# A two-layer decode kernel: chain pieces spread over the free steps, another closing block, and w2 loaded in rows of two

## The chip, the cores and the metric

The kernel runs on one core of a Trainium2 chip. A core has five engines with an instruction queue each: TensorE (PE: matrix products; its weight loads are listed as PEld), VectorE (DVE), ScalarE (ACT), GpSimd (POOL) and SyncE (SP, which issues nearly all transfers here). Data lies in HBM, is brought by 16 DMA engines into SBUF (128 partitions), and products are collected in PSUM banks. The metric is the device time of one execution in microseconds. Before the change it is 1165.13 us, the median of three runs (1164.89 to 1167.07).

## The reference

One token for each of 8 batch entries passes twice through an attention block and an MLP block, each with a layer norm ahead of it and a residual behind. Both passes use the same weights and the same caches.

```python
def _A_ref(x, k_cache, v_cache, wq, wo):          # B=8, D=512, 32 query heads, 8 KV heads, Sk=8192, Dh=128
    q = (x @ wq).reshape(B, Sq, Hq, Dh).transpose(0, 2, 1, 3)
    k = jnp.repeat(k_cache, rep, axis=1)
    v = jnp.repeat(v_cache, rep, axis=1)
    p = _softmax(jnp.einsum("bhqd,bhkd->bhqk", q, k) * (Dh ** -0.5), axis=-1)
    o = jnp.einsum("bhqk,bhkd->bhqd", p, v)
    return o.transpose(0, 2, 1, 3).reshape(B, Sq, Hq * Dh) @ wo

def _B_ref(x, w1, w2):                            # F=1792
    return jnp.einsum("bsf,fd->bsd", _silu(jnp.einsum("bsd,df->bsf", x, w1)), w2)

x = x + _A_ref(_layernorm(x), k_cache, v_cache, wq, wo)
x = x + _B_ref(_layernorm(x), w1, w2)
x = x + _A_ref(_layernorm(x), k_cache, v_cache, wq, wo)
x = x + _B_ref(_layernorm(x), w1, w2)
```

All of it is bf16. The two caches hold 134 MB each, so a pass over both is 268 MB.

## The kernel before

**Tasks and steps.** A task is the attention of one KV head group of one batch entry in one layer: 8192 keys, four query heads. There are 128 tasks, put in one order for the whole kernel by `make_tasks` (L159): layer 1 of a batch entry, later its layer 2, with tasks of other entries in between. A task has 8 steps of 1024 keys; the main loop (L918) runs over steps p. Each step transposes eight 128x128 blocks of K on TensorE (L538) and copies them back to SBUF on VectorE or ScalarE (L546, L544); every other step multiplies the queries with 2048 transposed keys (scores, L577), and the steps between multiply V with the probabilities (L643), 12 steps behind. Softmax lies between, on VectorE, GpSimd and ScalarE (L588 to L629), for each task at fixed steps.

**What is kept.** Five of the eight KV heads keep their transposed K in SBUF from layer 1 to layer 2, 20 blocks of 512 KB out of 28 slots; so the second layer loads less K. `plan_loads` (L200) fixes the order, the slot and the size (512 KB to 2 MB) of every load ahead of time, and the step after which its slot is free. SP issues them in this order (`issue_until`, L502), each behind a wait for the engines that last used the slot. The weights wo, w1 and w2 are loads in the same queue (L43, L505).

**The chain.** When the last layer-1 task of batch entry b is done, everything between its two attention layers follows in one chain of 22 pieces (`chain_of`, L828): the last two wo parts and the residual, seven pieces of the w1 products (L739) with the layer norm's operations beside them, the exponential and the Silu, four pieces of the w2 products with the residual, six pieces of the queries for three head groups with the second layer norm beside them, and the queries' scaling. The main loop takes one piece a step from this list (L942), as soon as there is one. Queries of the other five head groups (`asks`) follow only when the entry's layer-2 tasks have begun, and the wo parts of the next entry (`add_heads`) after that. The layer-2 tasks of entry b begin 30 steps after the chain's list is made, for the first and last entry 38.

**The layer norm in a chain** works on uncentered products and corrects them with column sums; its inverse root is a bit trick and three Newton steps on VectorE (`inverse_root`, L663).

**The closing** (`closing`, L776) does the last MLP for all eight entries at once: residual, sum over the features (VectorE and a GpSimd reduction over partitions, `total`, L684), centering, w1 products, centering again in fp32, square, second sum, inverse root in twelve VectorE operations, scaling, Silu, w2 products in four column quarters at once (`quads`, L780), and the store. `keep_busy` (L554) puts products of 512 columns on TensorE whose results nobody reads: four near the end of the last task (BEFORE) and six behind the w1 products (AFTER). A first Silu on a value that nobody reads (L789) makes ScalarE load the Silu table during the last task.

The planner's queue and the per-step order are all fixed when the kernel is built; the engines only wait on semaphores. `op` (L429) adds these waits by what an instruction reads and writes.

Of the kernel before, what the change touches and what calls it, by code (L numbers as in the profile page):

```python
# [9 lines left out]
LN_EPS = 1e-5  # L10
# [25 lines left out]
QSOON = 3  # L36
ASKS = (2, 5)
SUMS = 24
OPENING = 3
WEIGHTS = (("wo", 16), ("w1", 30), ("w2", 48))  # L40
NTP = 3
# [6 lines left out]
PVN = (12, 16)  # L48
CW = 32
AGAIN = 4  # L50
BEFORE, AFTER = 4, 6
ACT_EVAC = (0, 4, 6)

BF16 = mybir.dt.bfloat16
# [2 lines left out]
ACT = mybir.ActivationFunctionType  # L57
# [246 lines left out]
def _build(ctx, nc, A_x, A_k_cache, A_v_cache, A_wq, A_wo, B_w1, B_w2, out):  # L304
# [29 lines left out]
    def sb(shape, dt, name):  # L334
        _cnt[0] += 1
        return ctx.enter_context(nc.sbuf_tensor(f"{name}_{_cnt[0]}", shape, dt))
# [18 lines left out]
    w1_sb = sb([128, KT, F], BF16, "w1")  # L355
    w2_sb = sb([128, FT, D], BF16, "w2")
    ident = sb([128, 128], BF16, "ident")
    XT = [sb([128, KT, B], BF16, f"XT{n}") for n in range(3)]
    NQ = 128 // QUAD
    CPB = KB // 128  # L360
# [86 lines left out]
    def mm_group(steps, reads=(), writes=()):  # L447
        def run():
            inst = None
            for f in steps:  # L450
                inst = f()
            return inst
        return op(pe, run, reads, writes)
# [17 lines left out]
    with nc.Block() as block:  # L471

        @block.sync
        def _(sync_eng):
# [8 lines left out]
                ),  # L483
                reads=["ident"], writes=["ident"],
            )
            for n in range(NQB):
                op(pool, lambda n=n: pool.memset(QB[n], 0.0), writes=[f"QB{n}"])
            op(dve, lambda: dve.memset(one, 1.0), writes=["one"])
# [13 lines left out]
            def issue_until(pos):  # L502
                while queue and queue[0].after <= pos:
                    d = queue.pop(0)
                    if d.kind in weights:  # L505
                        src, dst = weights[d.kind]
                        dma(sp, dst[:, :, :], src.rearrange("(k p) n -> p k n", p=128), wsem[d.kind], writes=[d.kind])
                    else:
                        issue(d)

# [192 lines left out]

                return [lambda: total(xv, rx, 1), second] + inverse_root(1)

            def normed(xv, rx, w_sb, rw, outs, again=1):

                total(xv, rx, B)
                center(xbB, ["PT", "xb"], xv, rx, B)
                for f in project(w_sb, rw, outs, KT, lambda k: xbB[:, k, :], "xb", B, again=again):  # L710
                    f()
                if again > 1:
                    keep_busy(AFTER)
                center(xcB, ["xcB"], xv, rx, B)
                op(dve, lambda: dve.tensor_tensor(sqB, xcB, xcB, ALU.mult), reads=["xcB"], writes=["sqB"])
                total(sqB, "sqB", B)
                for f in inverse_root(B):
                    f()
# [7 lines left out]
            def project(w_sb, rw, outs, kparts, rhs_of, r_rhs, n, parts=1, again=1):  # L726

                steps = []
                w = CW if n == 1 else n * again

                def moved(k):
                    if n == 1:
                        return rhs_of(k).to_broadcast([128, w])
                    return rhs_of(k).unsqueeze(1).to_broadcast([128, again, n]) if again > 1 else rhs_of(k)

                for i, o in enumerate(outs):
                    for k in range(kparts):
                        steps.append(
                            lambda i=i, o=o, k=k: pe.matmul(  # L739
                                MISC[:, i * n:i * n + w] if again == 1 else  # L740
                                MISC[:, i * w:(i + 1) * w].rearrange("p (r b) -> p r b", b=n),
                                w_sb[:, k, o * 128:(o + 1) * 128], moved(k),
                                start=(k == 0), stop=(k == kparts - 1),
                            )
                        )
                cuts = [len(steps) * j // parts for j in range(parts + 1)]
                return [
                    lambda lo=lo, hi=hi: mm_group(steps[lo:hi], reads=[rw, r_rhs], writes=["MISC"])
                    for lo, hi in zip(cuts, cuts[1:])
                ]  # L750
# [24 lines left out]

            def closing(x0, x1, r0, r1):  # L776

                rows = SCp[0]

                def quads(lhs_of, rhs_of, parts, first, last):  # L780
                    return [
                        lambda k=k, c=c: pe.matmul(
                            rows[c * QUAD:c * QUAD + B, 0:128], lhs_of(k, c), rhs_of(k, c),
                            start=first, stop=last and k == parts - 1,
                        )
                        for k in range(parts) for c in range(KT)
                    ]

                op(act, lambda: act.activation(raw[:, 0:1], raw[:, 0:1], ACT.Silu), reads=["raw"], writes=["raw"])  # L789
                add_residual(x1, r1, x0, r0, B, B)  # L790
                mm_group(quads(lambda k, c: x1[:, c, :], lambda k, c: ident[:, :], 1, True, False),
                         reads=[r1, "ident"], writes=["SC0"])
                normed(x1, r1, w1_sb, "w1", range(FT), AGAIN)
                scaled(hB.rearrange("p (f b) -> p f b", b=B), ["P"], FT, AGAIN)
                op(act, lambda: act.activation(hsB, hB, ACT.Silu), reads=["P"], writes=["hsB"])
                mm_group(quads(lambda k, c: hsB[:, k * B:(k + 1) * B], lambda k, c: w2_sb[:, k, c * 128:(c + 1) * 128],
                               FT, False, True),
                         reads=["hsB", "w2"], writes=["SC0"])
                op(dve, lambda: dve.tensor_copy(P[:, 0:128], rows[:, 0:128]), reads=["SC0"], writes=["P"])
# [111 lines left out]
            setup = column_sums()  # L911
            chain_b = [None]
            turn = [0]
            last0 = {b: max(task_at[(0, b, g)] for g in range(HKV)) for b in range(B)}
            first1 = {b: min(task_at[(1, b, g)] for g in range(HKV)) * GPT for b in range(B)}
            ntask = len(tasks)

            for p in range(NG + LP + GPT + 1):  # L918
                tq = (p + LQ) // GPT
                if (p + LQ) % GPT == 0 and tq < ntask:  # L920
                    layer, b, _g = tasks[tq]
                    if layer == 1 and chain and chain_b[0] == b:
                        while chain:
                            chain.pop(0)()
                    emit_q(tq)
                emit_t_until(p + LT)
                if p % GPG == GPG - 1:
                    if p < NG:
                        emit_s(p)
                else:  # L930
                    for i in range(p - LP, p - LP + GPG):
                        if 0 <= i < NG:
                            emit_pv(i)
                ti, ph = p // GPT - 1, p % GPT
                if p == NG + 3:
                    keep_busy(BEFORE)
                if 0 <= ti < ntask and ph in soft:
                    for f in soft[ph]:
                        f(ti)
                if setup and p >= SUMS:  # L940
                    setup.pop(0)()
                elif chain:  # L942
                    left = max(1, first1[chain_b[0]] - EARLY - p)
                    for _n in range(2 if len(chain) > left else 1):
                        chain.pop(0)()
                elif asks and p >= first1[chain_b[0]]:
                    if p % GPT in ASKS:
                        asks.pop(0)()
                elif not setup and not asks and heads[turn[0]] and (p >= NG or turn[0] == B
                                         or p % GPG == GPG - 1 and (tasks[p // GPT][2], 0) in kept):  # L950
                    add_heads(turn[0])
                done = p - LP - GPT + GPG
                if done >= 0 and done % GPT == 0 and done // GPT < ntask:
                    tj = done // GPT
                    emit_norm(tj)
                    layer, b, _g = tasks[tj]
                    if layer == 0:
                        heads[b].append(_g)
                    elif b == B - 1:
                        heads[B].append(_g)  # L960
                    if layer == 0 and tj == last0[b]:
                        assert not setup and not chain and not asks and turn[0] == b
                        more, asks = chain_of(b)
                        chain.extend(more)
                        chain_b[0] = b
                        turn[0] = b + 1
                issue_until(p)
# [40 lines left out]
```

## Time and profile before

| | |
|---|---|
| median of three runs | 1165.13 us |
| the profiled execution: its time, its span | 1165.28 us, 1163.5 us |
| mean granted TensorE clock | 0.972 of full speed |
| TensorE busy / weight loads / VectorE / ScalarE / GpSimd | 83% / 65% / 51% / 33% / 10% |
| read from HBM | 465.05 MB, 400 GB/s over the span |
| last load of V lands, by the wait that it ends | 1152.3 us |

The span runs from the first to the last instruction. The slices show 40 equal parts of it, a digit for the busy share in tenths; a DMA share above 1 comes from packets that overlap on one engine. A row of the groups names line, engine, operation, output and inputs, shapes and count. In the timeline, the bracket says how long the engine was idle before the instruction and what ended it. In the stretches, the numbers behind the busy times are the granted clock, the DMA share and GB/s.

### The profile page before, as it was taken

The numbers are of one execution on the slowest core, as the hardware profiler recorded it, in microseconds if no ns is written. First come the engines' busy times: TensorE is split into PE (matmuls) and PEld (weight loads), VectorE is DVE, ScalarE is ACT, GpSimd is POOL, SyncE is SP. The second block draws the span as 40 slices with busy tenths as digits, with TensorE's granted clock in tenths as the row PEclk, the third lists the DMA queues.
The fourth block names the chain that finished last, engine by engine and source line by source line (L and its number), as shares of the span: only waits on it lengthen the run. The fifth ranks groups of instructions, "written<-read, shape, count | busy, mean of one in ns | idle before, by whom it ended". The sixth has DMA issues, their size and how long they took to land.

```text
span 1163.5 us, 44942 instructions
## 1 busy us (share of the span) xinstructions
PE 965.6 (83%) x19898; PEld 753.5 (65%) x19898; DVE 597.6 (51%) x1932; ACT 383.8 (33%) x660; POOL 118.1 (10%) x300
## 2 busy tenths in 40 slices
PE   4688887888878887989888887888879888888787
PEld 3577665677657665767666665667667666667565
DVE  2344564556545563556445654556446554556443
ACT  1223431343224331343234332343234322433232
POOL 0000011001100011001100111001100011001110
PEclk8789999999999999899999999999989998999998
DMA  9999999999999999999999999999999999999995
GB/s 367 388 418 402 406 405 413 423 400 404 412 423 414 387 405 419 420 393 407 410 420 409 397 405 422 415 396 404 403 422 413 395 408 421 419 392 397 410 411 212
DMA packets 100706, 467.98 MB, mean 402 GB/s; under 512 B 10520, under 2 KB 16416, under 8 KB 78624
## 3 DMA queue, kind: packets, MB, share of 16 engines
q1 hardware_dynamic: 100464, 465.09, 99.4%
q8 instruction: 157, 2.57, 0.9%
q14 instruction: 37, 0.30, 0.1%
q10 hardware_dynamic: 48, 0.01, 0.0%
HBM read 465.05 MB, written 0.01 MB: 400 GB/s over the span
## 4 chain that ended last, share of the span: by engine, by line
DMA 62%; PE 29%; DVE 3%; issue 2%; SPq 2%; ACT 2%; POOL 1%; ACTq 0%
DMA arena<-in_A_k_cache_dram 35%; DMA arena<-in_A_v_cache_dram 27%; PE TPp L538 10%; PE OTp L643 8%; PE SCp L577 5%; PE MISC L739 3%; SPq L443 2%; ACT P L602 2%; PE TPp L618 1%; PE MISC L758 1%; DVE small L588 1%; POOL small L592 1%; DVE PT L622 0%; DVE small L590 0%; DVE small L596 0%
## 5 line engine op out<-in xcount | busy, mean ns | idle before, releaser
L538 PE MATMUL TPp<-ident,arena 128*128 128x128 bf16 x5632 | 445.1, 223 | 86.1 <-DMA arena<-in_A_k_cache_dram 81.5
L546 DVE COPY arena<-TPp 128x1024 bf16<-128x1024 bf16 x440 | 303.8, 691 | 321.7 <-PE TPp L538 319.5
L538 PEld LDWEIGHTS TPp<-ident,arena 128*128 128x128 bf16 x5632 | 330.9, 99 | 154.1 <-DMA arena<-in_A_k_cache_dram 103.3
L544 ACT COPY arena<-TPp 128x1024 bf16<-128x1024 bf16 x264 | 267.0, 1012 | 305.2 <-PE TPp L538 305.2
L643 PE MATMUL OTp<-PT,arena 128*128 128x64 bf16 (+1 forms) x8192 | 317.4, 190 | 53.9 <-DMA arena<-in_A_v_cache_dram 31.0
L643 PEld LDWEIGHTS OTp<-PT,arena 128*128 128x128 bf16 x8192 | 273.6, 98 | 93.0 <-issue 48.0
L577 PE MATMUL SCp<-arena,QB 128*32 128x512 bf16 x2048 | 208.5, 397 | 10.0 <-DVE arena L546 4.3
L602 ACT ACTIVATE P<-SCp,small 128x512 bf16<-128x512 f32 x128 | 88.0, 687 | 387.8 <-DVE small L598 206.5
L592 POOL PARTITION_ALL_REDUCE small<-small x128 | 47.7, 373 | 713.9 <-DVE small L590 687.0
L588 DVE TENSOR_REDUCE small<-SCp 128x1 f32<-128x512 f32 x128 | 87.6, 684 | 40.2 <-PE SCp L577 39.2
L577 PEld LDWEIGHTS SCp<-arena,QB 128*32 128x32 bf16 x2048 | 54.1, 93 | 57.7 <-DVE arena L546 7.3
L610 POOL PARTITION_ALL_REDUCE small<-small x128 | 56.1, 438 | 236.3 <-DVE small L608 236.3
L622 DVE COPY PT<-TPp 128x256 bf16<-128x256 bf16 x128 | 37.3, 292 | 68.9 <-PE TPp L618 68.9
L618 PE MATMUL TPp<-ident,P 128*128 128x128 bf16 x512 | 51.2, 223 | 25.8 <-ACT P L602 25.8
L618 PEld LDWEIGHTS TPp<-ident,P 128*128 128x128 bf16 x512 | 29.1, 98 | 58.2 <-ACT P L602 44.5
L608 DVE TENSOR_SCALAR small<-small 128x4 f32<-128x4 f32 x128 | 29.2, 228 | 32.8 <-ACT P L602 32.2
L739 PE MATMUL MISC<-XT,wq 128*128 128x32 bf16 x1024 | 39.8, 177 | 1.0 <-issue 1.0
L739 PEld LDWEIGHTS MISC<-XT,wq 128*128 128x128 bf16 x1024 | 32.2, 96 | 8.4 <-issue 8.4
L758 PE MATMUL MISC<-at,wo 128*128 128x32 bf16 x1024 | 36.0, 177 | 1.6 <-issue 1.5
L758 PEld LDWEIGHTS MISC<-at,wo 128*128 128x128 bf16 x1024 | 31.6, 96 | 5.1 <-issue 5.1
L590 DVE SCALAR_TENSOR_TENSOR small<-small 128x4 f32<-128x4 f32 x128 | 28.5, 223 | 4.5
L596 DVE SCALAR_TENSOR_TENSOR small<-small 128x4 f32<-128x4 f32 x128 | 20.0, 156 | 20.4 <-POOL small L592 20.4
(69 smaller groups left out, 322.4 us busy)
## 6 DMA issues: line engine op xcount, KB each, us to landing
arena<-in_A_v_cache_dram SPq DMA_DIRECT2D x290, 512.0 KB, 8.3
arena<-in_A_v_cache_dram SPq DMA_DIRECT2D x111, 1024.0 KB, 11.4
arena<-in_A_k_cache_dram SPq DMA_DIRECT2D x192, 512.0 KB, 8.2
arena<-in_A_k_cache_dram SPq DMA_DIRECT2D x24, 2048.0 KB, 15.0
arena<-in_A_k_cache_dram SPq DMA_DIRECT2D x32, 1024.0 KB, 14.8
wq<-in_A_wq_dram SPq DMA_DIRECT2D x1, 4096.0 KB, 16.8
wo<-in_A_wo_dram SPq DMA_DIRECT2D x1, 4096.0 KB, 27.8
w<-in_B_w_dram SPq DMA_DIRECT2D x2, 1792.0 KB, 26.8
```

What stands on the lines that cost most here:

```text
L538: lambda c=c: pe.transpose(tpv[:, c, :], chunk(slot, h * GRP + c), ident[:, :])
L544: op(act, lambda: act.copy(dst, TPp[tb][:, :]), reads=[f"TP{tb}"], writes=[r_half(slot, h)])
L546: op(dve, lambda: dve.tensor_copy(dst, TPp[tb][:, :]), reads=[f"TP{tb}"], writes=[r_half(slot, h)])
L577: lambda c=c: pe.matmul(SCp[bank][c * QUAD:(c + 1) * QUAD, :], QB[qn][:, NGRAN - 1 - k:NGRAN - 1 - k + QUAD], ARENA[:, slot * SLOT + c * K ...
L588: op(dve, lambda: dve.tensor_reduce(rowmax, SCp[bank][:, :], AX.X, ALU.max), reads=[f"SC{bank}"], writes=["rowmax"])
L592: op(pool, lambda: pool.partition_all_reduce(tops, top, 128, bass.bass_isa.ReduceOp.max), reads=["top"], writes=["tops"])
L602: op(act, lambda: act.activation(P[:, :], SCp[bank][:, :], ACT.Exp, bias=shift, scale=SM_SCALE, accum_out=rs[st]), reads=[f"SC{bank}", "sh ...
L610: op(pool, lambda: pool.partition_all_reduce(ssa[st], ssm[st], 128, bass.bass_isa.ReduceOp.add), reads=[f"ssm{st}"], writes=[f"ssa{st}"])
L618: lambda c=c: pe.transpose(tpv[:, c, :], P[:, c * 128:(c + 1) * 128], ident[:, :])
L643: lambda c=c, cc=cc: pe.matmul(otp, chunk(slot, h * GRP + c), pv[:, cc % CPB, cc // CPB % NQ, k, :].unsqueeze(2).to_broadcast([128, REP, w ...
L739: lambda i=i, o=o, k=k: pe.matmul(MISC[:, i * n:i * n + w] if again == 1 else MISC[:, i * w:(i + 1) * w].rearrange("p (r b) -> p r b", b=n ...
L758: lambda o=o, h=h: pe.matmul(MISC[:, o * w:(o + 1) * w], wo_sb[:, h, o * 128:(o + 1) * 128], rhs_of(h).to_broadcast([128, w]) if n == 1 el ...
```

## The change

Three things are changed.

The main loop counts, when a chain begins, the steps left until two before the entry's first layer-2 task, and takes so many pieces at each step that they are spread evenly: 22 pieces over 27 steps, or over 35 for the first and the last entry.

The closing block takes the means from TensorE: x1 is multiplied with a block of ones, which a memset writes over a used part of wq at step NG + 1. The variance is the mean of squares minus the square of the mean; ScalarE squares, VectorE and GpSimd sum. The inverse root is exp(-0.5 ln v) on ScalarE, with a table set that holds both functions and is loaded at the kernel's start. The Silu table is loaded behind them. `keep_busy` has two products ahead of w1 and three behind it.

w2 comes into SBUF so that each partition gets two neighbouring rows of w2 (2 KB) at a time: 7 x 128 pieces of 2 KB instead of 14 x 128 of 1 KB. The hidden features then lie in another order, so the w1 products read every second column of w1.

```diff
+FC = 2
+LN_EXP = 6
-BEFORE, AFTER = 4, 6
+BEFORE, BETWEEN, AFTER = 4, 2, 3
...
+    ones = wq_sb[:, KT - 1, 0:128]
...
+            act.add_instruction(mybir.InstLoadActFuncSet(
+                name=nc.get_next_instruction_name(), act_func_set_id=LN_EXP, ins=[], outs=[]))
...
+                        if d.kind == "w2":
+                            dst = dst[:, :, :].rearrange("p (a c) d -> p a (c d)", c=FC)
+                            src = src.rearrange("(a p c) d -> p a (c d)", p=128, c=FC)
...
+                def columns(k, o):
+                    if rw == "w1":
+                        lo = o // FC * FC * 128 + o % FC
+                        return w_sb[:, k, lo:lo + FC * 127 + 1:FC]
+                    return w_sb[:, k, o * 128:(o + 1) * 128]
...
-                op(act, lambda: act.activation(raw[:, 0:1], raw[:, 0:1], ACT.Silu), reads=["raw"], writes=["raw"])
                 add_residual(x1, r1, x0, r0, B, B)
+                mm_group([lambda k=k: pe.matmul(means[:, 0:B], ones[:, :], x1[:, k, :], start=(k == 0), stop=(k == KT - 1))
+                          for k in range(KT)], reads=[r1, "wq"], writes=["SC1"])
                 mm_group(quads(lambda k, c: x1[:, c, :], lambda k, c: ident[:, :], 1, True, False),
                          reads=[r1, "ident"], writes=["SC0"])
-                normed(x1, r1, w1_sb, "w1", range(FT), AGAIN)
+                op(act, lambda: act.activation(sqB, x1, ACT.Square), reads=[r1], writes=["PT", "sqB"])
+                op(dve, lambda: dve.tensor_reduce(s1, sqB.rearrange("p k b -> p b k"), AX.X, ALU.add),
+                   reads=["sqB"], writes=["s1"])
+                op(pool, lambda: pool.partition_all_reduce(s1a, s1, 128, bass.bass_isa.ReduceOp.add),
+                   reads=["s1"], writes=["s1a"])
+                keep_busy(BETWEEN)
+                op(dve, lambda: dve.scalar_tensor_tensor(
+                    xbB, means[:, 0:B].unsqueeze(1).to_broadcast([128, KT, B]), -1.0 / D, x1, op0=ALU.mult, op1=ALU.add),
+                   reads=["SC1", r1], writes=["PT", "xb"])
+                project(w1_sb, "w1", range(FT), KT, lambda k: xbB[:, k, :], "xb", B, again=AGAIN)[0]()
+                keep_busy(AFTER)
+                op(act, lambda: act.activation(tr, means[:, 0:B], ACT.Square, scale=1.0 / D), reads=["SC1"], writes=["tr", "SC1"])
+                op(dve, lambda: dve.scalar_tensor_tensor(s1a, s1a, 1.0 / D, tr, op0=ALU.mult, op1=ALU.subtract),
+                   reads=["s1a", "tr"], writes=["s1a"])
+                op(dve, lambda: dve.tensor_scalar(s1a, s1a, 0.0, LN_EPS, op0=ALU.max, op1=ALU.add),
+                   reads=["s1a"], writes=["s1a"])
+                op(act, lambda: act.activation(tr, s1a, ACT.Ln), reads=["s1a"], writes=["tr"])
+                op(act, lambda: act.activation(yr, tr, ACT.Exp, scale=-0.5), reads=["tr"], writes=["yr"])
+                op(act, lambda: act.activation(raw[:, 0:1], raw[:, 0:1], ACT.Silu), reads=["raw"], writes=["raw"])
                 scaled(hB.rearrange("p (f b) -> p f b", b=B), ["P"], FT, AGAIN)
...
+                if p == NG + 1:
+                    op(dve, lambda: dve.memset(ones, 1.0), writes=["wq"])
...
                     left = max(1, first1[chain_b[0]] - EARLY - p)
-                    for _n in range(2 if len(chain) > left else 1):
+                    span[0] = max(span[0], left)
+                    for _n in range(max(0, len(chain) - span[1] * (left - 1) // span[0])):
                         chain.pop(0)()
...
+                        span[:] = [0, len(chain)]
```

More of the change, by code (lines that the diff above doesn't have):

```diff
@@ L506, in issue_until @@
                         src, dst = weights[d.kind]
[L507 removed]
+                        if d.kind == "w2":
+                            dst = dst[:, :, :].rearrange("p (a c) d -> p a (c d)", c=FC)
+                            src = src.rearrange("(a p c) d -> p a (c d)", p=128, c=FC)
+                        else:
+                            dst, src = dst[:, :, :], src.rearrange("(k p) n -> p k n", p=128)
+                        dma(sp, dst, src, wsem[d.kind], writes=[d.kind])
                     else:
@@ L704, in ln_stages, with normed @@
                 return [lambda: total(xv, rx, 1), second] + inverse_root(1)
-            def normed(xv, rx, w_sb, rw, outs, again=1):
+            def normed(xv, rx, w_sb, rw, outs):
                 total(xv, rx, B)
                 center(xbB, ["PT", "xb"], xv, rx, B)
-                for f in project(w_sb, rw, outs, KT, lambda k: xbB[:, k, :], "xb", B, again=again):
+                for f in project(w_sb, rw, outs, KT, lambda k: xbB[:, k, :], "xb", B):
                     f()
-                if again > 1:
-                    keep_busy(AFTER)
                 center(xcB, ["xcB"], xv, rx, B)
@@ L741, in project @@
                                 MISC[:, i * w:(i + 1) * w].rearrange("p (r b) -> p r b", b=n),
-                                w_sb[:, k, o * 128:(o + 1) * 128], moved(k),
+                                columns(k, o), moved(k),
                                 start=(k == 0), stop=(k == kparts - 1),
@@ L776, in closing @@
             def closing(x0, x1, r0, r1):
-                rows = SCp[0]
+                rows, means = SCp
                 def quads(lhs_of, rhs_of, parts, first, last):
@@ L913, in _ @@
             turn = [0]
+            span = [0, 0]
             last0 = {b: max(task_at[(0, b, g)] for g in range(HKV)) for b in range(B)}
```

## The prediction

> **What bounds the kernel now.** I read the page from the top: busy shares first, then the slices.
>
> ```profile
> PE 965.6 (83%) x19898; PEld 753.5 (65%) x19898; DVE 597.6 (51%) x1932; ACT 383.8 (33%) x660; POOL 118.1 (10%) x300
> ...
> DMA  9999999999999999999999999999999999999995
> ...
> q1 hardware_dynamic: 100464, 465.09, 99.4%
> ```
>
> TensorE is busy 83% of the span, but the DMA engines are full in every slice except the last. So the question is whether loads are ever short of requests. The DMA issues of the page give the depth of the queue:
>
> ```profile
> arena<-in_A_v_cache_dram SPq DMA_DIRECT2D x290, 512.0 KB, 8.3
> ...
> arena<-in_A_k_cache_dram SPq DMA_DIRECT2D x192, 512.0 KB, 8.2
> ```
>
> 512 KB at 408 GB/s take 1.29 us, and a load lands 8.2 us after its issue: some six loads are under way at any time. Next, stretches of the span: one ahead of a chain (the rows of line L739 with w1 put the chain of the second batch at 270 us), three with a chain in them, one behind a chain.
>
> ```profile
> core 0: us, PE busy (x) PEld busy (x) DVE busy (x) ACT busy (x) POOL busy (x), PEclk, DMA share, GB/s
> 225.00:265.00 40.00, 35.41 (x688) 28.05 (x689) 22.01 (x56) 16.56 (x25) 3.44 (x9) 1.00 1.01 405
> 270.00:298.00 28.00, 24.86 (x559) 20.14 (x556) 18.91 (x77) 10.13 (x17) 3.59 (x9) 1.00 1.02 404
> 425.00:465.00 40.00, 30.86 (x689) 22.33 (x685) 18.14 (x67) 8.37 (x21) 4.83 (x12) 0.99 1.02 416
> 657.00:683.00 26.00, 23.30 (x528) 18.93 (x525) 16.75 (x70) 10.08 (x16) 3.19 (x8) 1.00 1.03 405
> 1045.00:1072.00 27.00, 24.02 (x548) 19.67 (x546) 17.76 (x73) 10.06 (x16) 3.32 (x9) 1.00 1.03 402
> ```
>
> A chain adds work to TensorE and VectorE (18.91 us of VectorE in 28, against 22.01 in 40), and the DMA share stays above 1.00 at the rate of the stretch ahead of it. Up to the last load the time is bytes over rate. The last load lands at 1152.3 us; what follows is serial, and the timeline shows it:
>
> ```profile
> start us, us, engine line op out<-in xcount [idle before <-releaser]
> ...
> 1152.36 0.57 PE L643 MATMUL OTp<-PT,arena 128*128 128x48 bf16 x16 [0.67 <-DMA arena<-in_A_v_cache_dram]
> ...
> 1153.82 0.19 DVE L770 TENSOR_TENSOR XT<-MISC,XT 128x32 bf16<-128x32 f32 x1 [0.68 <-PE MISC L758]
> ...
> 1154.35 0.41 POOL L687 PARTITION_ALL_REDUCE small<-small  x1 [4.37 <-DVE small L685]
> ...
> 1155.04 1.68 PE L739 MATMUL MISC<-PT,w 128*128 128x32 bf16 x56 [0.69 <-DVE PT L691]
> ...
> 1156.09 0.17 DVE L668 TENSOR_SCALAR small<-small 128x8 f32<-128x8 f32 x1 [0.54 <-POOL small L687]
> ...
> 1158.90 0.30 ACT L795 ACTIVATE PT<-P 128x112 bf16<-128x112 f32 x1 [8.20 <-DVE P L721]
> ...
> 1159.25 1.67 PE L782 MATMUL SCp<-w,PT 128*8 128x128 bf16 x56
> ```
>
> Between 1154.01 (end of the residual) and 1159.25 (start of the w2 products) VectorE sets the pace: two reductions through GpSimd and twelve small operations of 0.17 us at a pitch of 0.20 for the inverse root (1156.09 to 1158.49), then scaling, Silu. The w1 products were done at 1156.72 and waited.
>
> **The change, part by part.** The sum is made against the profiled execution: span 1163.54, time 1165.28 (1.74 lie around the span), 0.15 above the median of 1165.13.
>
> *The spread.* Before, a chain's 22 pieces took one step each from the step after the last wo part became known; now they lie over 27 steps (batches 1 to 6) or 35 (batches 0 and 7). No piece is added: every matmul, VectorE operation and the two GpSimd reductions of each layer norm stay, in the same order among themselves, later against the transposes and softmax. SP's order is unchanged, and each load's wait names transposes, scores or PV work, not the chain. The last piece (queries of the first groups) comes 4 steps before its layer-2 task instead of 8 (16 for the long ones), some 5 us by a step of 1.3 (a chain's seven w1 pieces span 8.1 us); it needs 0.22 + 0.24 us of VectorE, so ScalarE's copy into QB finds it done. Price: 0. What hides it is the queue of six loads, 8 us deep; with that cover gone, up to a step of 1.3 us per batch could show, 10 us in all. From the other side: if the chain stretches ran at the 416 GB/s of the stretch behind, 8 x 27 us x (1 - 404/416) = 6.2 us would be gained. I take 0, since the nearest row, the stretch ahead without a chain, has 405.
>
> *w2 in rows of two.* 1,792 packets of 1 KB become 896 of 2 KB. The row of the stretch where w2 passes:
>
> ```profile
> 84.00:87.00 3.00, 2.70 (x64) 2.37 (x65) 2.14 (x7) 0.78 (x2) 0.37 (x1) 1.00 1.02 426
> 87.50:93.50 6.00, 5.00 (x122) 4.30 (x119) 1.76 (x4) 2.46 (x4) 0.34 (x1) 1.00 1.08 365
> ```
>
> The slices inside it, where only w2 passes, show 349 GB/s: 1.835 MB take 5.26 us. At the 405 of 4 KB packets they would take 4.53. By packet, sixteen at a time, 1 KB costs 46.9 ns and 4 KB 162 ns; the line between gives 85 ns for 2 KB, 4.77 us in all. Gain 0.49; ends 0 and 0.73. The engines are full there, so it moves the last load by as much.
>
> *The stride in w1.* To match, the w1 columns of a hidden block are read two apart, in the 504 w1 weight loads of setup and chains and the 56 of the closing. The trace has no strided weight load. Its rows with 128 columns in a row step by 26.7 ns a pair (w1 at 1155.04: 56 in 1.50 us plus 0.18 of drain). Bounds: 26.7, and four times that, 107 ns. I take 26.7: the same 26.7 stands under clock 1.00 (L758, 8 columns moved) and 0.50, so the read has a pace of its own, and the nearest row is the same load without stride.
>
> [...]
>
> *Small edits.* ScalarE's table load moves to the start, where ScalarE waits 5.1 us for the first K: 0. The memset of 128x128 for the ones (GpSimd's like it: 0.20 us) stands on VectorE between L590 and L596, under the 0.37 us of the GpSimd reduction at 1147.57, five us ahead of the last load: 0.
>
> *The closing,* from the residual's end at 1154.01, with gaps as in the timeline (VectorE to TensorE 0.05, to GpSimd 0.09, others 0.03 to 0.04):
> - ScalarE squares x1 (32 elements; 14 take 0.215, 112 take 0.296): 0.23, to 1154.28. VectorE waits for it with its reduction (0.21, to 1154.52), and the centering queued behind waits too: 0.20, to 1154.75. GpSimd: 0.41, from 1154.61 to 1155.02.
> - TensorE: four products with ones, four with the identity, then two fillers of 0.427 (their pitch at clock 0.50) from about 1154.28: they end at 1155.13, later than the centering. So w1 starts at 1155.13, 0.09 later than before, and its results are there at 1156.8.
> - ScalarE squares the means behind the centering (PSUM bank SC1 is held for it): to 1154.99. VectorE: two operations, to 1155.42. Ln and Exp at 0.21: to 1155.90. That replaces a second reduction and twelve operations.
> - The Silu table load (1.28, row L789) was hidden at 1149.2 and now stands behind Exp: 1155.92 to 1157.20, and the first Silu to 1157.42.
> - Scaling is done at 1157.10 (w1 + 0.28), so it waits for ScalarE; Silu ends at 1157.75. The three fillers behind w1 end at 1157.90 at clock 0.50. w2 starts at 1157.80 to 1157.90 instead of 1159.25: gain 1.34.
>
> *The clock.* In this execution the granted clock was 0.50 in the whole closing:
>
> ```profile
> 1154.00:1157.40 3.40, 2.64 (x63) 1.91 (x64) 2.02 (x13) 0.00 (x0) 0.82 (x2) 0.50 0.00 0
> 1157.40:1160.80 3.40, 3.40 (x61) 1.79 (x59) 1.19 (x7) 0.30 (x1) 0.00 (x0) 0.50 0.00 0
> ...
> 464.50:467.90 3.40, 2.74 (x32) 2.11 (x33) 2.01 (x6) 0.00 (x0) 0.37 (x1) 0.50 1.02 431
> 467.90:471.30 3.40, 3.40 (x41) 2.77 (x39) 1.13 (x4) 1.77 (x3) 0.43 (x1) 0.50 0.98 405
> 471.40:474.70 3.30, 3.30 (x72) 2.74 (x70) 1.76 (x4) 1.11 (x2) 0.00 (x0) 1.00 1.04 437
> ```
>
> It changes in steps of 3.41 us, and a stretch at 0.50 that is 3.40 busy is followed by 1.00, one with 2.64 or 2.74 is not. The two fillers close the gap from 1154.35 to 1155.04, so the stretch from 1154.0 becomes about 3.3 busy and the clock should be back at 1157.4, ahead of w2. The w2 products are 14 rounds of 107 ns at 0.50 and of 53 ns at 1.00: 0.75 less. The sum: 0.49 + 1.34 + 0.75 = 2.58, 1165.28 - 2.58 = **1162.7 us**.
>
> **The rivals.** Measurement tells 0.2% (2.3 us) from no change, so small terms decide the sign.
> 1. *The clock's steps fall otherwise.* Then w2 stays at 0.50: 1165.28 - 1.83 = 1163.4, within 0.2%. For it: a step needs to begin within about 1 us of 1154.1, out of 3.41. Against: in the profiled execution it did. [...]
> 2. *The spread does move the stream,* at half of the 6.2 us above: about 1159.6. For it: TensorE waits 81.5 us for K over the run. Against: DMA share above 1.00 in every chain stretch.
> 3. *Strided weights at 53 ns.* w1 ends at 1155.13 + 2.97 + 0.18 = 1158.28, w2 starts at 1159.0: gain 0.25 there, 0.49 from w2: 1164.5, within 0.2%.
> 4. *Slower: strided weights at 107 ns.* w1 ends at 1161.3, w2 starts at 1162.0, 2.75 late; less 0.49 is +2.3; each chain holds TensorE 56 x 80 ns = 4.5 us longer, half the queue, and a microsecond per two batches gets through: 4. About 1171. Up to 34 ns a pair costs nothing (w1 done by 1157.1), from 68 ns the closing and w2 gain nothing. For it: no row shows such loads.
>
> **Chances.** Forecast 0.36 (its own range 1161.8 to 1163.6; 0.28 beyond 0.2%, 0.08 within), rival 1 0.25 (0.06 beyond, 0.19 within), rival 2 0.12 (faster), rival 3 0.10 (within), rival 4 0.17 (slower, a starved stream by the spread included). Faster 0.46, same 0.37, slower 0.17. The range 1161.0 to 1165.0 takes in rivals 1 and 3 and leaves out 4 and most of 2.
>
> **What would show it.** The last load lands 0.5 us earlier (1151.8) with chain stretches still at 402 to 408 GB/s; w1's 56 loads take 1.5 us; the ACT table load stands at about 2.9 us behind the last PV; from the residual's end to the start of w2 it takes 3.8 us instead of 5.2. It is wrong if w1 steps by more than 34 ns, if the DMA share drops below 1.00 in a chain, or if the Silu table load ends later than 1.3 us behind Exp.

## The result

The changed kernel takes 1164.41 us (median of 22 runs, 1162.40 to 1167.86) against 1166.46 us for the kernel before in the same sessions (22 runs, 1164.82 to 1168.17): ratio 0.9984, 95% interval 0.9979 to 0.9990, so 1.9 us less, between 1.2 and 2.4. Measured again later beside another set of runs of the kernel before, the ratio was 0.9993 (0.9984 to 1.0001); the two intervals overlap, and the change is worth about 0.07% to 0.16%. The profiled execution took 1165.14 us with a span of 1163.32.

The page of the changed kernel, the lines that answer to those of before:

```profile
PE 970.5 (83%) x19898; PEld 758.8 (65%) x19901; DVE 594.6 (51%) x1920; ACT 384.6 (33%) x664; POOL 117.5 (10%) x299
...
DMA  9999999999999999999999999999999999999996
...
q1 hardware_dynamic: 99568, 465.09, 99.4%
...
arena<-in_A_v_cache_dram SPq DMA_DIRECT2D x290, 512.0 KB, 8.0
...
arena<-in_A_k_cache_dram SPq DMA_DIRECT2D x192, 512.0 KB, 8.2
```

The shares are the same, the packets are 896 fewer, and a load of 512 KB still lands some 8 us after its issue. Stretches of the changed kernel (columns as before: busy times, granted clock, DMA share, GB/s), first the one in which w2 passes:

```profile
core 0: us, PE busy (x) PEld busy (x) DVE busy (x) ACT busy (x) POOL busy (x), PEclk, DMA share, GB/s
87.50:93.50 6.00, 4.73 (x114) 4.08 (x112) 1.84 (x5) 2.12 (x3) 0.43 (x1) 1.00 1.05 398
...
225.00:265.00 40.00, 35.35 (x700) 28.26 (x698) 22.26 (x56) 16.91 (x27) 3.20 (x8) 1.00 1.02 407
270.00:298.00 28.00, 24.24 (x534) 19.48 (x531) 17.41 (x66) 10.16 (x16) 3.59 (x9) 1.00 1.02 401
...
425.00:465.00 40.00, 31.82 (x701) 23.25 (x702) 17.73 (x73) 8.37 (x21) 4.83 (x12) 0.97 1.02 417
661.00:687.00 26.00, 23.42 (x524) 18.86 (x522) 17.14 (x64) 10.05 (x16) 3.59 (x9) 1.00 1.00 382
1048.00:1075.00 27.00, 23.01 (x502) 18.38 (x498) 17.04 (x61) 9.94 (x18) 2.79 (x7) 1.00 1.03 408
```

With w2 the rate is 398 instead of 365 GB/s. With a chain it is 401 and 408, where it was 404 and 402. One chain stretch stands out: 661 to 687 ran at 382 GB/s with a DMA share of 1.00, where the kernel before had 405 and 1.03 (657 to 683). Just ahead of it the granted clock was 0.50, from 656.84 to 660.26. In the second profile of the changed kernel the same stretch has 398 GB/s at 1.02, and with the spread alone 403 at 1.02. So the slow stretch is one profile's, and the two others with the same spread do not have it. The closing, in the timeline of the changed kernel:

```profile
start us, us, engine line op out<-in xcount [idle before <-releaser]
...
1155.90 0.19 DVE L785 TENSOR_TENSOR XT<-MISC,XT 128x32 bf16<-128x32 f32 x1 [0.68 <-PE MISC L773]
1156.12 0.23 ACT L809 ACTIVATE PT<-XT 128x32 f32<-128x32 bf16 x1 [5.01 <-DVE XT L785]
...
1156.68 0.41 POOL L812 PARTITION_ALL_REDUCE small<-small  x1 [4.79 <-DVE PT L815]
...
1156.93 1.56 PE L754 MATMUL MISC<-PT,w 128*128 128x32 bf16 x56
1157.12 0.17 DVE L821 SCALAR_TENSOR_TENSOR small<-small 128x8 f32<-128x8 f32 x1 [0.43 <-POOL small L812]
...
1157.53 0.21 ACT L825 ACTIVATE small<-small 128x8 f32<-128x8 f32 x1 [0.57 <-DVE small L823]
1157.77 0.21 ACT L826 ACTIVATE small<-small 128x8 f32<-128x8 f32 x1
1157.99 1.28 ACT L827 ACT_TABLE_LOAD   x1
...
1159.40 0.28 ACT L829 ACTIVATE PT<-P 128x112 bf16<-128x112 f32 x1
1159.73 0.95 PE L797 MATMUL SCp<-w,PT 128*8 128x128 bf16 x56 [0.58 <-ACT PT L829]
```

One reduction on GpSimd instead of two, then Ln, Exp, the Silu table load, Silu. From the residual's end (1156.09) to the start of the w2 products it takes 3.64 us, before 5.23. The products take 0.95 us instead of 1.67, since the granted clock is 1.00 in the whole closing here. The last load lands 2.1 us later than in the execution shown of before (1154.4 against 1152.3), which eats most of that in this one execution; the last section comes back to it.

### The profile page after: what moved, and what is told of

It is laid out like the page before. It is cut to its first block, busy times and chain, and to the rows that moved or that the text cites. A ratio compares the mean times of both kernels' runs of the same rounds, so it can differ in the third digit from the quotient of the medians.

```text
span 1163.3 us, 44939 instructions
## 1 busy us (share of the span) xinstructions
PE 970.5 (83%) x19898; PEld 758.8 (65%) x19901; DVE 594.6 (51%) x1920; ACT 384.6 (33%) x664; POOL 117.5 (10%) x299
## 4 chain that ended last, share of the span: by engine, by line
DMA 64%; PE 25%; DVE 3%; issue 2%; SPq 2%; ACT 2%; POOL 1%; POOLq 0%; ACTq 0%
DMA arena<-in_A_k_cache_dram 33%; DMA arena<-in_A_v_cache_dram 31%; PE TPp L548 9%; PE OTp L653 8%; PE SCp L587 4%; SPq L446 2%; ACT P L612 2%; PE MISC L754 2%; PE TPp L628 1%; DVE small L598 1%; PE MISC L773 1%; POOL small L602 1%; DVE small L600 0%; DVE PT L632 0%; DVE arena L556 0%
## 5 line engine op out<-in xcount | busy, mean ns | idle before, releaser
L548 PEld LDWEIGHTS TPp<-ident,arena 128*128 128x128 bf16 x5632 | 334.6, 100 | 152.3 <-DMA arena<-in_A_k_cache_dram 101.1
```

The costliest lines, as they stand in the source:

```text
L548: lambda c=c: pe.transpose(tpv[:, c, :], chunk(slot, h * GRP + c), ident[:, :])
```

## The experiments

Each kernel ran beside the kernel before; ratios are to that kernel's runs on the same chip, with a 95% interval.

### The spread alone

The kernel before with the changed lines of the main loop.

```diff
-                    for _n in range(2 if len(chain) > left else 1):
+                    span[0] = max(span[0], left)
+                    for _n in range(max(0, len(chain) - span[1] * (left - 1) // span[0])):
```

> The kernel before with the spread of the chain alone. If the transfers bound everything up to the last load (my theory): ratio 0.9995 to 1.0005, the closing as before (5.2 us from the residual's end to the start of the w2 products, if the clock is at 0.50), chain stretches at 400 to 408 GB/s. If the spread moves the stream (rival 2): ratio 0.997 to 0.9985, that is 2 to 3 us, and the last load lands earlier by as much. If the later end of the chain costs something: ratio over 1.001.

Measured: ratio 1.0005 (0.9996 to 1.0013). The gain of 2 to 3 us of rival 2 lies outside the interval. The closing took 5.21 us to the start of w2, as before. The stretches of this kernel with chains:

```profile
270.00:298.00 28.00, 24.11 (x535) 19.40 (x532) 17.37 (x65) 10.16 (x16) 3.46 (x9) 1.00 1.02 400
400.00:426.00 26.00, 23.68 (x528) 19.20 (x524) 17.11 (x65) 10.16 (x16) 3.22 (x8) 1.00 1.03 408
```

The spread is worth nothing that this interval shows.

### The chain crowded: two and four pieces at each step

Is that because placement never matters, or because one piece a step is already mild enough? The opposite edit, on the kernel before:

```diff
-                    for _n in range(2 if len(chain) > left else 1):
+                    for _n in range(min(len(chain), 4)):
```

> The kernel before with up to four pieces of a chain at each step instead of one, so that the 22 pieces stand within 6 steps. If the six loads under way hide any placement of the chain: ratio 0.9995 to 1.001 and a DMA share of 1.00 or more in the chain stretches. If placement matters, this is the harsher case: some 6 us of waits and products pile up in each of 8 chains, 2 to 4 us a chain get past the queue: ratio 1.01 to 1.03.

Measured: 1.0367 (1.0348 to 1.0385), 1208.07 us: 42 us more, 5.3 per chain, over the 2 to 4 expected if placement matters. And with 2 in place of 4:

> The kernel before with two pieces of a chain at each step, 11 steps, between one a step (before) and four (1.0367 measured). If there is a sharp edge where the queue runs dry: two a step still fits, ratio 0.9995 to 1.003. If the cost grows with the crowding: some 14 us, ratio 1.008 to 1.016.

Measured: 1.0208 (1.0186 to 1.0231), 1190.83 us: 25 us more, 3.1 per chain, above both expectations. One chain of each, first four pieces a step, then two:

```profile
275.00:280.00 5.00, 3.55 (x102) 3.02 (x98) 3.67 (x21) 1.01 (x1) 0.80 (x2) 1.00 1.01 392
280.00:285.00 5.00, 3.73 (x109) 3.30 (x110) 2.24 (x12) 0.76 (x3) 0.38 (x1) 1.00 0.78 278
285.00:290.00 5.00, 4.04 (x106) 3.49 (x102) 4.13 (x18) 0.55 (x1) 0.76 (x2) 1.00 0.70 220
```

```profile
275.00:280.00 5.00, 3.89 (x100) 3.33 (x100) 4.06 (x20) 2.03 (x4) 0.40 (x1) 1.00 1.02 401
280.00:285.00 5.00, 3.56 (x101) 3.13 (x102) 3.08 (x13) 0.78 (x2) 0.41 (x2) 1.00 0.91 345
285.00:290.00 5.00, 4.54 (x115) 3.81 (x111) 2.94 (x18) 2.13 (x3) 1.15 (x3) 1.00 0.85 292
```

The DMA share falls to 0.70 and 0.85 a few microseconds after the crowded pieces begin, while TensorE is not full either. What it waits for stands in the waits of the four-piece kernel between 270 and 290 us:

```profile
PE MISC L739 <- DVE small L847: 2.2, 1, 2.2
```

The pieces depend on each other through VectorE and GpSimd. Where they follow each other on TensorE without enough attention work between, TensorE waits for VectorE with the next transposes queued behind it: between 275 and 300 us it waits 4.7 us for VectorE in this kernel (2.2 in the row above, 2.0 for copies of K, 0.5 for the residual), and in the kernel before not at all. The slots come free late: from 274.3 to 285 us SP issues four loads, and in the kernel before eight. The six loads under way run out. At one piece a step that does not happen, and 27 steps instead of 22 then have nothing to save.

### w2 in rows of two alone, and wider rows

The kernel before with w2 in rows of two and w1 read two apart.

```diff
+                            dst = dst[:, :, :].rearrange("p (a c) d -> p a (c d)", c=FC)
+                            src = src.rearrange("(a p c) d -> p a (c d)", p=128, c=FC)
...
-                                w_sb[:, k, o * 128:(o + 1) * 128], moved(k),
+                                columns(k, o), moved(k),
```

> The kernel before with w2 in rows of two, and so w1 read with stride two, alone. My theory: the w2 slices go from 349 to about 385 GB/s, the last load moves by 0.5 us, w1's 56 loads in the closing still take 1.5 to 1.6 us: ratio 0.9993 to 0.9999. If strided weight loads cost 53 ns a pair (rival 3): the closing's w1 takes 3 us, still hidden behind the inverse root, chains 1.5 us of TensorE each: ratio near 1.000. At 107 ns (rival 4): closing 2 to 3 us longer, ratio 1.002 to 1.005.

Measured: 0.9996 (0.9988 to 1.0005), w2's stretch at 392 GB/s, and in the slices where only w2 passes 385 to 390 instead of 349: 4.7 us instead of 5.26. Then the changed kernel with rows of fourteen and of seven, so the same step between w1's columns:

```diff
-FC = 2
+FC = 14
```

> The changed kernel with w2 in rows of fourteen (128 pieces of 14 KB) and w1 therefore read with a stride of fourteen columns. If the weight load has a pace of its own that stride does not touch (my theory): w1's 56 loads in the closing still step by 25 to 28 ns, the slices with w2 reach 410 to 425 GB/s, 0.3 us off the last load, ratio to the kernel before 0.998 to 0.9988, like the change. If a wider stride costs: 53 to 107 ns a pair, w1 ends 1.5 to 4.5 us later in the closing and the ratio is 0.9985 to 1.002.

> The changed kernel with rows of seven, so a stride of seven columns (14 bytes) in w1's weight loads; two columns cost nothing (25 to 28 ns a pair), fourteen cost 60. If the cost sets in with a byte distance beyond 16: 25 to 28 ns. If it grows with the stride: about 40 ns, or 60 as with fourteen.

Measured: rows of fourteen 0.9999 (0.9990 to 1.0007), rows of seven 1165.81 us in one run. The w1 weight loads of the closing (ns: min/median/max), steps of two, seven and fourteen in this order:

```profile
L754 PEld LDWEIGHTS MISC<-PT,w x56: 96/97/98, 1156.7 to 1158.3; 128*128 128x128 bf16 x56
```

```profile
L754 PEld LDWEIGHTS MISC<-PT,w x56: 131/153/153, 1155.2 to 1158.2; 128*128 128x128 bf16 x56
```

```profile
L754 PEld LDWEIGHTS MISC<-PT,w x56: 153/162/164, 1154.7 to 1158.3; 128*128 128x128 bf16 x56
```

From start to start the products take 25.1 ns with a step of two, 52.9 with seven, 59.9 with fourteen (1.37, 2.91 and 3.29 us for 55). The closings with seven and fourteen ran largely at clock 0.50; in the chains, at full clock, the median step is the same, 53 and 60 ns. A step of two is free (at clock 0.50 the 56 products take 1.70 us with it, in the Newton kernel below, and 1.70 with columns next to each other, in the closing alone), rival 3's 53 ns came true for a step of seven, and of my two cases for fourteen the one that I held with (25 to 28 ns) was wrong. With fourteen w1 holds the closing: in this profile w2 starts 6.01 us behind the residual's end. The Silu is done at 5.44, and the three fillers, late behind w1, hold w2 for the rest. The closing alone, which met clock 0.50 too, takes 3.93 (below), and the change at full clock 3.64. That takes the whole gain back. So the stride would have undone the change, had the rows been fourteen wide.

### The closing alone

The changed kernel with rows of one and the old main loop.

```diff
-FC = 2
+FC = 1
...
-                    for _n in range(max(0, len(chain) - span[1] * (left - 1) // span[0])):
+                    for _n in range(2 if len(chain) > left else 1):
```

> The kernel before with the new closing block, the table set at the start and the fillers, but neither the spread nor the rows of two. My theory: 3.7 to 3.9 us from the residual's end to the start of the w2 products instead of 5.2, ratio 0.998 to 0.9992 (1 to 2.3 us by the clock that w2 meets). If the spread is what gained: ratio near 1.000.

Measured: 0.9984 (0.9976 to 0.9993), 1163.62 us, and 3.93 us to the start of w2. That is the same ratio as the whole change's; the 0.5 us of w2's rows is smaller than either interval. The residual, the fillers behind w1, the Silu and w2:

```profile
1154.18 0.19 DVE L785 TENSOR_TENSOR XT<-MISC,XT 128x32 bf16<-128x32 f32 x1 [0.68 <-PE MISC L773]
...
1157.19 1.18 PE L568 MATMUL TPp<-wq,ident 128*128 128x512 bf16 x3
...
1157.70 0.30 ACT L829 ACTIVATE PT<-P 128x112 bf16<-128x112 f32 x1
...
1158.30 0.95 PE L797 MATMUL SCp<-w,PT 128*8 128x128 bf16 x56
```

The Silu ends at 1158.00, and w2 starts at 1158.30, when the fillers are through: at clock 0.50 they cost 0.30 us ahead of w2.

### What in the closing gains

The bit trick and three Newton steps instead of Ln and Exp, with the Silu table loaded ahead again:

```diff
-                op(act, lambda: act.activation(tr, s1a, ACT.Ln), reads=["s1a"], writes=["tr"])
-                op(act, lambda: act.activation(yr, tr, ACT.Exp, scale=-0.5), reads=["tr"], writes=["yr"])
-                op(act, lambda: act.activation(raw[:, 0:1], raw[:, 0:1], ACT.Silu), reads=["raw"], writes=["raw"])
+                for f in inverse_root(B, True):
+                    f()
```

> The changed kernel with the bit trick and three Newton steps in place of Ln and Exp, and the Silu table load hidden ahead of the residual again. It keeps the means on TensorE and the single GpSimd sum. My theory: eleven operations at a pitch of 0.20 us end 3.6 us behind the residual, w2 starts at 4.2 to 4.4 instead of 3.6 to 3.9: of the 1.3 to 1.6 us gained in the closing some 0.9 come from the sums and 0.5 from Ln and Exp, which pay for the table load of 1.28. Ratio 0.9985 to 0.9992. If Ln and Exp are the whole gain: w2 starts at 5.2 again, ratio 0.9995 to 1.000.

Measured: 0.9990 (0.9981 to 0.9999), w2 starts 4.38 us behind the residual's end, as expected. Its timeline has the residual, the first and the last operation of the root, and w2:

```profile
1154.78 0.19 DVE L786 TENSOR_TENSOR XT<-MISC,XT 128x32 bf16<-128x32 f32 x1 [0.68 <-PE MISC L774]
...
1156.41 0.17 DVE L681 TENSOR_SCALAR small<-small 128x8 int32<-128x8 int32 x1
...
1158.43 0.17 DVE L690 SCALAR_TENSOR_TENSOR small<-small 128x8 f32<-128x8 f32 x1
...
1159.36 0.95 PE L798 MATMUL SCp<-w,PT 128*8 128x128 bf16 x56 [0.61 <-ACT PT L830]
```

Of the 1.59 us between 5.23 and 3.64, 0.85 come from the means on TensorE and the single sum, 0.74 from Ln and Exp with their table load on the path. This split is read from single profiles; the times of the two kernels overlap. It also mixes clocks: the Newton kernel met 0.50 in its closing, and the 3.64 stands at 1.00. Against the closing alone, which met 0.50 too, Ln and Exp gain 0.71 us to the end of the Silu, and 0.45 to the start of w2, since the fillers hold w2 there.

The sum of squares on TensorE as well, in a PSUM bank that is free by then:

```diff
-                op(act, lambda: act.activation(sqB, x1, ACT.Square), reads=[r1], writes=["PT", "sqB"])
-                op(dve, lambda: dve.tensor_reduce(s1, sqB.rearrange("p k b -> p b k"), AX.X, ALU.add),
-                   reads=["sqB"], writes=["s1"])
-                op(pool, lambda: pool.partition_all_reduce(s1a, s1, 128, bass.bass_isa.ReduceOp.add),
-                   reads=["s1"], writes=["s1a"])
+                op(act, lambda: act.activation(sq16, x1, ACT.Square), reads=[r1], writes=["PT", "sqB"])
+                mm_group([lambda k=k: pe.matmul(OTp[0][:, 0:B], ones[:, :], sq16[:, k, :], start=(k == 0), stop=(k == KT - 1))
+                          for k in range(KT)], reads=["sqB", "wq"], writes=["OT0"])
```

> The changed kernel with the sum of squares on TensorE too (ones against bf16 squares, into a PSUM bank that the PV work no longer uses), without the VectorE and GpSimd sums. The sum on GpSimd ended 1.0 us behind the residual's end; without it the variance should be there at 0.95, Exp end at 1.6 instead of 1.9, the Silu table load 0.3 earlier, w2 start at 3.3 to 3.4. Ratio to the kernel before 0.998 to 0.9988, a shade under the change. If the products of the squares delay w1 behind them on TensorE: w1 starts 0.2 later, still ahead of the Silu table, no loss.

Measured: 0.9988 (0.9979 to 0.9997), w2 starts at 3.57, not at 3.3 to 3.4. Its timeline shows why:

```profile
1156.27 0.19 DVE L785 TENSOR_TENSOR XT<-MISC,XT 128x32 bf16<-128x32 f32 x1 [0.68 <-PE MISC L773]
...
1156.86 0.19 DVE L814 SCALAR_TENSOR_TENSOR PT<-SCp,XT 128x32 bf16<-128x32 f32 x1 [0.40 <-PE SCp L805]
...
1157.14 0.18 ACT L819 ACTIVATE small<-SCp 128x8 f32<-128x8 f32 x1 [0.42 <-PE OTp L811]
1157.42 0.17 DVE L820 SCALAR_TENSOR_TENSOR small<-OTp,small 128x8 f32<-128x8 f32 x1 [0.37 <-ACT small L819]
```

The sum was no longer late; the square of the means was (ACT L819), behind the means' products and the centering. The bracket names the products of the squares, which end at 1157.12; by the kernel this operation does not read them but waits for the centering, which ends at 1157.05. In the changed kernel two paths met within 0.15 us at that subtraction (1156.96 and 1157.09), so taking one away gained 0.07. The changed kernel ran beside it:

> The changed kernel again, beside the one with the squares on TensorE: ratio to the kernel before 0.998 to 0.999 as on record, w2 start 3.6 to 3.9 us behind the residual's end by the clock of the closing.

Measured: 0.9993 (0.9984 to 1.0001), again 3.64 us. No version here is clearly ahead of the changed kernel.

### The fillers and the clock

The changed kernel without the products that only keep TensorE busy.

```diff
-                keep_busy(BETWEEN)
...
-                keep_busy(AFTER)
```

> The changed kernel without the two fillers ahead of the w1 products and the three behind them. If the fillers bring the clock back for w2 (my theory of the clock): the stretch behind the residual is at most 2 us busy in 3.4, the clock is at 0.50 for the w2 products in most executions, 107 ns a round instead of 53, so the median is 0.4 to 0.75 us higher: ratio to the kernel before 0.9985 to 0.9995. If the clock's steps fall at random whatever the fillers do: ratio as the change, 0.998 to 0.9987. The start of w2 stays 3.6 to 3.9 us behind the residual's end in both.

Measured: 0.9985 (0.9976 to 0.9994), which cannot be told from the change by its time. In its profile w2 met clock 0.50 and took 1.67 us. Two stretches of the closing, first of the kernel with the closing alone (with fillers), then of the one without:

```profile
1154.60:1158.00 3.40, 3.40 (x69) 2.17 (x65) 0.92 (x5) 2.34 (x7) 0.41 (x1) 0.50 0.00 0
1158.10:1161.30 3.20, 1.16 (x58) 0.77 (x56) 0.29 (x1) 0.00 (x0) 0.00 (x0) 1.00 0.04 8
```

```profile
1152.90:1156.20 3.30, 2.41 (x80) 2.05 (x77) 1.11 (x6) 1.55 (x5) 0.41 (x1) 1.00 0.02 5
1156.30:1159.70 3.40, 1.67 (x56) 1.38 (x56) 0.29 (x1) 0.84 (x3) 0.00 (x0) 0.50 0.02 5
```

In the closing alone, with fillers, a stretch at 0.50 is full and one step later the clock is back at 1.00, just ahead of w2, as the prediction had it. In the changed kernel it went otherwise: in both of its profiles the clock did not fall until w2 was through. And the kernel before, too, has w2 at full clock more often than its shown execution says. From the start of w2 to the cast behind it:

| closing | us from the start of w2 to the cast, one profile each |
|---|---|
| before (kernel before, spread alone, rows of two alone, four and two pieces a step) | 1.72, 1.11, 1.01, 1.24, 1.04 |
| new, with fillers, w1 at 25 to 28 ns (change twice, closing alone, Newton, squares) | 1.01, 1.01, 1.01, 1.01, 1.01 |
| new, without fillers | 1.72 |
| new, with fillers, w1 at 53 and 60 ns | 1.72, 1.52 |

The old closing met the slow clock for all of w2 in one of five profiles, and that one was the execution shown. The mean gain of the clock is 0.2 us (1.22 - 1.01), not 0.71. From the residual's end to the cast, the five old closings take 6.22 to 6.95 us, on average 6.44, the change takes 4.65 both times, and the kernel without fillers 5.36.

Do the fillers do it, or only the point at which the clock's steps of 3.41 us happen to fall? Four profiles have nearly the same point, counted back from the clock's next fall. The table has the step that begins just ahead of the residual's end:

| kernel | the step begins, us from the residual's end | TensorE busy in it, of 3.41 us at clock 1.00 | clock in the next step |
|---|---|---|---|
| the change | -0.89 | 2.83 | 1.00 |
| the change again | -0.60 | 3.13 | 1.00 |
| squares on TensorE | -0.75 | 3.12 | 1.00 |
| without fillers | -0.71 | 2.46 | 0.50 |

At this point the fillers go with the clock being kept, three profiles against one. The busy time alone is not the rule, though: in all four the step ahead was busy for only 2.24 to 2.30 us, and the clock stayed. Nor is a full step at 0.50 always followed by 1.00: with rows of seven and of fourteen TensorE's rows fill one (3.41 of 3.41 us, from 1155.46 and 1154.10), and the next step was at 0.50 again. The reason stays open.

## Why the prediction was right, and what it missed

The measured 1164.41 us lies inside the stated range. But the forecast of 1162.7 was counted from 1165.28, one execution, and the kernel before measured 1166.46 over 22 runs: of the 1.7 us between forecast and result 1.2 is this base, and 0.5 the gain. That the time still fell inside the range is in part luck.

1. *The bound.* Right. In the profiles of both kernels the DMA engines are 90% busy or more in every slice but the last; nothing that the change moved ahead of the last load showed in the times.
2. *The spread: 0.* Right, 1.0005 (0.9996 to 1.0013). One sign of being wrong that I named for it, a DMA share below 1.00 in a chain, was met in one profile of the changed kernel: 0.92 from 660.26 to 663.70 and 0.98 to 667, at the head of the stretch with 382 GB/s and right behind a fall of the clock. The change again and the spread alone do not show it. Its cover, the six loads under way, was named and is real: crowding the chain used it up, at 3.1 and 5.3 us a chain. The price I gave for a lost cover, up to one step of 1.3 us a batch, was too small by a factor of two to four for these crowded chains.
3. *w2: 0.49 us.* Right for w2's own transfer: 349 to 385 or more GB/s, 0.5 us. The time of that kernel alone, 0.9996 with 0.9988 to 1.0005, fits but does not show it. Nor does the sign named for it, a last load at 1151.8: it landed at 1154.4 and 1152.8 in the two profiles of the change, and the stream varies by more than 0.5 us.
4. *The stride of two: nothing.* Right, 25.1 ns a pair at full clock, where the forecast had 26.7. The runs show that a step of seven or fourteen costs 2.1 and 2.4 times as much; why, they do not show. The 53 ns of rival 3 and the 107 ns of rival 4 were assumed values, twice and four times 26.7, and no run shows either for a step of two. 53 ns was the real price of another stride, a step of seven (52.9); 107 ns was met nowhere, the widest step measured costs 59.9.
5. *The closing: 1.34 us at clock 0.50.* Right. The closing alone at 0.50 took 3.93 us, 1.30 less than 5.23, and at full clock the change took 3.64. Small steps were off and cancelled: the centering did not wait for the reduction's end but started 0.12 us behind its start, and the Silu began inside the first Silu's 0.20 us, so that in the closing alone the Silu ended 3.63 us behind the residual instead of 3.74. The two fillers ahead of w1 began 0.46 us behind the residual instead of 0.27, and so the fillers behind w1 let w2 start at 3.93, where the forecast had 3.79 to 3.89.
6. *The clock: 0.75 us.* This is the term that failed. In the changed kernel w2 did run at full clock, though not by the way forecast: the clock never fell there, where I had a stretch at 0.50 filled and the clock back one step later. The closing alone and the Newton kernel went the way forecast. The rule behind it, a full stretch at 0.50 is followed by 1.00, failed with rows of seven and fourteen (3.41 of 3.41 us busy, and 0.50 again). And I took the kernel before from a single execution whose draw (the point at which the clock's steps fell) was the worst of five. The term measures 0.2, from five profiles against five. With it the sum is 0.5 + 1.3 to 1.6 + 0.2 = 2.0 to 2.3 us, against 1.9 (1.2 to 2.4) measured; the 1.8 from the residual's end to the cast (6.44 - 4.65) and the 0.5 of w2 give the same. The forecast of 2.58 was too far by this term, and so the change ended within 0.2%, where rival 1 had put it. Rival 1 has the size right and the reason half: the clock's steps did fall otherwise than in the execution shown of before, but w2 did not stay at 0.50 in the two profiles of the change (1.01 us to the cast in both). How the point of the steps comes about is not shown; the five old closings, from 1.01 to 1.72 us, show only that it differs between executions.

## What to carry to other kernels

With a DMA share of 1.00 or more in the chain stretches and some six loads under way, spreading the moved work changed nothing here (1.0005), while crowding it ran the queue dry and cost 25 us at two pieces a step and 42 us at four. Crowding on purpose tells how near that edge is, which an average does not. Behind the last load everything was serial here (5.23 us from the residual's end to w2), and short operations at 0.20 us each were the cost: replacing twelve of them and a partition sum paid for a table load of 1.28 us that came onto the path. A term that hangs on the granted clock is to be taken over several profiles, not from the one at hand: it was 0.71 us by the execution shown and 0.2 us over five.

## What the runs showed of the hardware

- A weight load of 128 columns with its product takes 25 to 27 ns with columns next to each other or two apart, 52.9 ns seven apart (14 bytes) and 59.9 ns fourteen apart. The cost does not wait for a distance of 16 bytes, which was one of the two cases that I had set up.
- The stream itself varies by 3 us from one execution to the next: the residual behind the last load of V starts at 1153.37 us in one profile (without fillers) and at 1156.27 in another (squares on TensorE), with the same loads. In the changed kernel's profile much of it is one place:

```profile
500.00:510.00 10.00, 7.59 (x95) 5.79 (x92) 3.92 (x11) 2.65 (x4) 0.80 (x2) 0.66 0.99 384
510.00:520.00 10.00, 9.62 (x202) 7.97 (x200) 5.98 (x15) 3.95 (x7) 0.80 (x2) 1.00 0.87 307
```

  The granted clock averaged 0.66 in the first ten microseconds, and the DMA share fell to 0.87 in the next, with TensorE nearly full while it caught up. The kernel before had clock 1.00 and a DMA share of 1.01 in both. In order of time TensorE first waited 2.41 us for a load of V, up to 503.99, with a DMA share of 1.00; the clock was 0.50 from 503.25 to 510.07; the share fell below 0.99 only after that, to 0.93 and then 0.82. So the share did not fall ahead of the clock. That the clock emptied the queue is not shown: in the kernel before it was 0.50 just as long from 464.5, and the share stayed at 0.98 to 1.04.
